# A gated mix of a spectral filter and a gelu layer on one core: the instruction order as a list of steps, gate weights by GpSimd's queue, no zero products

## The chip, the cores and the metric

The kernel runs on one core of one Trainium2 chip. The metric is the device time of one execution in microseconds (us); a lower time is better. A kernel is timed in several runs, and its median counts. Besides, one execution is profiled; that execution has a time of its own, and its span (from the first to the last instruction) is a little shorter than this time.

The engines are called as the profile calls them: PE (TensorE, matrix products), PEld (its weight loads, which run beside the products), DVE (VectorE), ACT (ScalarE), POOL (GpSimd) and SP (SyncE, which only issues transfers). SP, ACT and POOL each have a queue from which transfers start.

## The reference, cut to what matters

```
def _A_ref(x, w_r, w_i):            # x: 1 x 2048 x 512
    X = rfft2(x, axes=(-2, -1))
    X = X * (w_r + 1j * w_i)        # 2048 x 257
    return irfft2(X, s=(2048, 512), axes=(-2, -1))

def _B_ref(x, w1, b1, w2, b2):      # w1: 512 x 1792, w2: 1792 x 512
    return gelu(x @ w1 + b1) @ w2 + b2

g = sigmoid((x * gate_w).sum(-1, keepdims=True))
out = g * _A_ref(x) + (1 - g) * _B_ref(x)
```

All arrays are float32.

## The kernel before, in words

**Products with split operands.** PE multiplies in a rounded float format. To keep float32 accuracy most operands are split: `h` is the operand rounded to 12 bits (an ACT copy), `l` is the rest (a DVE subtraction), and a product is made as hh + hl + lh, three PE instructions. A 128x512 tile product is one PE instruction of 512 columns. So behind almost every PE result stand an ACT and a DVE instruction before PE can use it again.

**The spectral half.** The 2048 rows are taken as 16 groups `j` of 128. For each `j` the function `forward` folds the row (`eo`, `w`, on DVE), makes the transform along the 512 columns by PE (`pd`, with the table `cf`, lines 676-685), splits the result (`zb`, lines 695 and 698), and makes the first transform step along the rows (`py`, with `tf`, lines 705-715). The two columns of the table `cf` that are left over carry the gate weights, so the same `pd` product gives the gate's logit; a tile `g3` holds the gate weights, and five tiny DVE instructions turn it into the columns of `cf` (lines 614-622). The rest of the transform along the rows, the filter and the way back are radix-4 steps on DVE (`radix4`, `filt`, `stage4`; lines 756-868); one small product `pown` (line 742) stands between them. `inverse` scales by the gate (`tg`), mixes the two halves (`pq` on DVE, line 901), multiplies (`pz`, `pa`) and adds the result.

**The gelu half.** Columns `c` = 0 and 1 of the row groups go through `mlp`: twelve 512-column products into a PSUM tile `ph` (line 1007 and after), gelu on ACT (line 995), the split into `g..h` and `g..l` (lines 557, 558), and three products per weight tile into `po`. This is done in passes over the 14 blocks `f` of the hidden layer; sums of the passes are added in DRAM by an adding transfer on POOL's queue (line 498). Columns 2 and 3 go through `fast`, which saves products by a seven-product scheme (Strassen's kind): `nu` and `ux` are its PSUM tiles, and `ux` is written by an ACT copy first and then added to by PE (line 1185). Before these copies, two products with a zero operand (`zerob`, lines 1168-1171) fill the two `ux` tiles once.

**PSUM.** There are eight tiles of one bank: four of kind `pf` (`pd`, `nu`, `pz`, `pa`) and four of kind `pm` (`ph`, `po`, `py`, `ux`). A tile that is given to a new owner waits for the last reader of the old one.

**What sets the order.** All work is first recorded as 2016 steps, each with an engine, the tiles that it reads and writes, a cost and a lag. `Graph.schedule` then plays a list scheduler: whenever an engine is free it takes, of the steps whose inputs are there and for whose tiles a buffer is free, the one with the lowest rank. The ranks are a table of numbers (`RANKS`), and `most` limits how many buffers a class of tiles holds. Costs, lags, a reserve of 0.4 for what PE waits for (`SPARE`) and a look ahead of 0.35 (`AHEAD`) take part. The plan gives every step its place and every tile its buffer number. The steps are then written out in this order, each engine gets its own in this order, and on the chip each engine goes through its list one by one: an instruction that waits holds up all that stand behind it on its engine.

**The start.** SP issues the first weight tile `war0` (two halves), the gate weights (`g3`, line 600), the second row tile `xf4` (two halves), and so on; ACT's queue issues the first row tile `xf0`. PE runs products on a zero tile (`none`) until data is there: six of 512 columns and `FILL` = 8 of 256 columns (lines 573-587).

Of the kernel before, what the change touches and what calls it, by code (L numbers as in the profile page):

```python
# [11 lines left out]
F32 = mybir.dt.float32  # L12
F32R = mybir.dt.float32r
AF = mybir.ActivationFunctionType
ALU = mybir.AluOpType
# [104 lines left out]
SPARE = 0.4  # L120

AHEAD = {"vec": 0.35, "act": 0.35}
# [5 lines left out]
RANKS = """  # L128
# [78 lines left out]
"""  # L207


# [1168 lines left out]
```

## Time and profile before

| what | value |
|---|---|
| median of 3 runs | 367.2 us (366.71 to 367.24) |
| the profiled execution, its own time | 368.04 us |
| its span | 366.2 us |
| busy: PE, DVE, ACT, POOL | 358.7, 327.8, 256.7, 69.6 us |
| granted TensorE clock, mean | 0.999 |
| moved by the 16 DMA engines | 70.35 MB, 192 GB/s in the mean |

How to read it: "busy" is the union of an engine's instructions. PE's instructions overlap in a pipeline, so a row of one product reads 0.39 us while the next one starts 0.227 us later; what a product costs is the distance to the next. A row of the timeline has the start, the duration, the engine, the line, the operation, the tiles (output<-input, without buffer numbers) and how often it stands there in a row; an idle time before it and what ended it may follow. A row of the waits has the engine and line that waited, what it waited for, and the sum in us, the number of times and the longest. A row of the windows has the busy time and the number of instructions of each engine in a stretch, then the granted clock, the share of the DMA engines and GB/s.

### The profile page before, as it was taken

The page shows a single profiled execution, that of the slowest core. Times are in us where ns is not written, and L with a number is a line of the kernel's source. Part 1 is how long each engine was busy: PE and PEld are TensorE (multiplying, and loading weights), DVE is VectorE, ACT ScalarE, POOL GpSimd, SP SyncE. Part 2 cuts the span into 40 slices and gives each one's busy share as a digit, 9 for nine tenths or more (in the row PEclk, how much of TensorE's full clock was granted, in tenths as well). Part 3 has the DMA queues.
Part 4 walks back from the last instruction along what each step waited for, and adds up shares of the span by engine and source line. Part 5 has one row for each costly group of instructions (what it writes and reads, how often), then busy time and mean ns, then how long its engine had stood idle before and what let it go on. Part 6 is the DMA issues. An engine that isn't in the chain of part 4 may idle for free.

```text
span 366.2 us, 5746 instructions
## 1 busy us (share of the span) xinstructions
PE 358.7 (98%) x1808; PEld 302.9 (83%) x1808; DVE 327.8 (90%) x746; ACT 256.7 (70%) x471; POOL 69.6 (19%) x89
## 2 busy tenths in 40 slices
PE   8999999999999999999999999999999999999994
PEld 8888898898878778878888788888888888888884
DVE  5999988998759999899999999999999769899962
ACT  4985778789986241753759975999999998655200
POOL 0210001100211311410333100002333112121220
PEclk9999999999999999999999999999999999999999
DMA  7999785647885937999999943339887637799896
GB/s 224 306 322 303 253 233 166 106 149 233 206 204 129 189 58 155 273 263 365 196 153 217 264 85 117 86 122 225 126 141 150 100 64 156 173 296 241 199 250 184
DMA packets 46719, 70.35 MB, mean 192 GB/s; under 512 B 5600, under 2 KB 19424, under 8 KB 46688
## 3 DMA queue, kind: packets, MB, share of 16 engines
q1 hardware_dynamic: 34880, 48.93, 41.8%
q0 software_dynamic: 11376, 20.71, 35.3%
q10 hardware_dynamic: 432, 0.33, 0.3%
q8 instruction: 14, 0.23, 0.3%
q14 instruction: 17, 0.14, 0.1%
HBM read 48.32 MB, written 19.41 MB: 185 GB/s over the span
## 4 chain that ended last, share of the span: by engine, by line
PE 75%; DVE 12%; DMA 5%; ACT 4%; issue 2%; SPq 1%; DVEq 0%; ACTq 0%
PE poB L507 20%; PE po L507 13%; PE ph L507 11%; PE ux L1185 9%; PE nu L1185 7%; PE pd L507 4%; PE pz L507 3%; PE py L507 3%; PE pa L507 3%; DVE m L856 3%; DMA wf<-in_wf 3%; DMA y<-ownr 1%; DMA xf<-in_xt 1%; DVE y L760 1%; DVE y L758 1%
## 5 line engine op out<-in xcount | busy, mean ns | idle before, releaser
L995 ACT ACTIVATE ph<-ph,b1t 128x512 f32<-128x512 f32 x28 | 18.4, 658 | 25.5 <-PE ph L507 25.2
L498 POOL DMA_DIRECT2D bacc<-o x16 | 15.3, 1029 | 43.2 <-ACT o L1073 43.2
L894 ACT ACTIVATE sw<-y,al 64x512 f32<-64x512 f32 x32 | 22.8, 718 | 0.6
L498 POOL DMA_DIRECT2D bacc<-oB x16 | 13.9, 889 | 43.0 <-ACT oB L1073 33.7
L856 DVE TENSOR_TENSOR m<-y,wf 128x514 f32<-128x514 f32 x32 | 20.7, 688 | 0.0
L507 PE MATMUL pd<-cf,w 128*128 128x129 f32 x128 | 17.7, 276 | 0.0
L507 PEld LDWEIGHTS pz<-tg,pq 128*128 128x128 f32 x128 | 16.8, 191 | 1.1
L507 PEld LDWEIGHTS pd<-cf,w 128*128 128x128 f32 x128 | 16.6, 191 | 1.2 <-DVE zb L698 0.3
L1185 PE MATMUL nu<-xf,wa0h 128*128 128x512 f32 x56 | 17.3, 390 | 0.0
L507 PE MATMUL pz<-tg,pq 128*128 128x128 f32 x128 | 17.2, 274 | 0.0
L507 PE MATMUL py<-zb,tf 128*128 128x258 f32 x96 | 17.1, 295 | 0.0
L723 ACT ACTIVATE y<-pys 64x257 f32<-64x257 f32 x32 | 13.2, 417 | 3.9 <-DVE pys L720 3.4
L507 PE MATMUL pa<-zb,ci 128*128 128x256 f32 x96 | 15.2, 285 | 0.2 <-ACT od L935 0.2
L507 PEld LDWEIGHTS pa<-zb,ci 128*128 128x128 f32 x96 | 13.8, 189 | 1.9 <-ACT od L935 0.7
L507 PEld LDWEIGHTS py<-zb,tf 128*128 128x128 f32 x96 | 14.1, 190 | 1.2 <-ACT pys L716 0.2
L1073 ACT ACTIVATE o<-po 128x512 f32<-128x512 f32 x16 | 9.2, 593 | 8.3 <-PE po L507 8.2
L901 DVE SCALAR_TENSOR_TENSOR pq<-y,al,sw 128x256 f32<-128x256 f32 x32 | 14.4, 479 | 0.0
L695 ACT ACTIVATE zb<-pd 128x256 fp32r<-128x256 f32 x32 | 11.6, 384 | 3.9 <-PE py L507 3.9
L698 DVE TENSOR_TENSOR zb<-pd,zb 128x256 fp32r<-128x256 f32 x32 | 12.5, 417 | 1.1 <-ACT zb L695 1.1
L665 DVE TENSOR_TENSOR w<-eo 128x256 f32<-128x256 f32 x32 | 12.8, 418 | 0.0
L662 DVE TENSOR_TENSOR eo<-xf 128x256 f32<-128x256 f32 x32 | 12.4, 419 | 0.0
L1185 PEld LDWEIGHTS nu<-xf,wa0h 128*128 128x128 f32 x56 | 10.5, 188 | 2.2
(701 smaller groups left out, 1274.3 us busy)
## 6 DMA issues: line engine op xcount, KB each, us to landing
wf<-in_wf SPq DMA_DIRECT2D x16, 257.0 KB, 4.7
bacc<-o POOLq DMA_DIRECT2D x16, 256.0 KB, 6.1
bacc<-oB POOLq DMA_DIRECT2D x16, 256.0 KB, 4.9
xf<-in_xt SPq DMA_DIRECT2D x14, 256.0 KB, 5.0
wr<-in_w SPq DMA_DIRECT2D x14, 256.0 KB, 4.9
tf<-tf SPq DMA_DIRECT2D x16, 192.0 KB, 2.8
bacc<-o SPq DMA_DIRECT2D x8, 256.0 KB, 3.2
ba<-bacc SPq DMA_DIRECT2D x8, 256.0 KB, 4.1
```

The source lines that it names most:

```text
L498: return add("pool", 2.3 * kb / 340, 3.4, lambda: nc.gpsimd.dma_start(dst(), src(), accum_op=ALU.add), reads, writes, rank)
L507: pe.matmul(ps, w, x, start=start, stop=stop)
L662: v(lambda s=s, op=op: vec.tensor_tensor(eo.ap()[:, s], x.ap()[:, 0:2], x.ap()[:, 2:4], op=op), 256, [x], [(eo, s)], feed)
L665: v(lambda s=s, op=op: vec.tensor_tensor(w.ap()[:, s], eo.ap()[:, :, 0], eo.ap()[:, :, 1], op=op), 256, [eo], [(w, s)], feed)
L695: a(lambda c=c: act.activation(segs(xh, c), both(c), AF.Copy), 256, [ps[c]], [(xh, c)], 0)
L698: v(lambda c=c: vec.tensor_tensor(segs(xl, c), both(c), segs(xh, c), op=ALU.subtract), 256, [ps[c], (xh, c)], [(xl, c)], 0)
L723: a(lambda o=o, i=i: act.activation(Y[j].ap()[o:o + HP, 1], pys.ap()[i:i + HP, 1], AF.Copy), 257, [(pys, 1)], [(Y[j], 1 + k)], 0, more=0.1)
L856: v(lambda mk=mk, k=k, y=y, w=w: vec.tensor_tensor(mk.ap(), y.ap(), w.ap()[:, k:k + 1, :ND].to_broadcast([P, 2, ND]), op=ALU.mult), 514, [ ...
L894: a(lambda sw=sw, y=y, o=o, i=i: act.activation(sw.ap()[o:o + HP], y.ap()[i:i + HP, ::-1, :HD], AF.Copy, scale=al.ap()[i:i + HP, 0:1]), 51 ...
L901: v(lambda sw=sw, pq_=pq_, y=y, j=j, k=k, op=op: vec.scalar_tensor_tensor(pq_.ap()[:, k], y.ap()[:, k, :HD], al.ap()[:, 1 + j:2 + j], sw.a ...
L995: a(lambda: act.activation(ps.ap(), ps.ap(), AF.Gelu_apprx_tanh, bias=b1t.ap()[:, f:f + 1]), 600, [b1t], [ps]).table = "gelu"
L1185: pe.matmul(o.ap(), w(wi, e), FX[j].ap()[:, xi, e], start=first, stop=k == 5, skip_group_check=not start)
```

## The change

The list scheduler goes, with `RANKS`, `most`, `SPARE` and `AHEAD`. In its place stand two tables: `ORDER`, the numbers of the 2015 steps in the order in which they are written out, and `SLOTS`, the buffer number of each tile. `schedule` now only gives out these numbers and asserts that every step comes after those it needs and that a buffer is free when it is given away. The order is another one throughout, on every engine; the products, copies and transfers in it are the same but for these:

- the gate weights `g3` and the bias `b1t` are issued by POOL's queue instead of SP's;
- `FILL` is 10 instead of 8: two more products on the zero tile at the start;
- the two products with a zero operand into `ux` go, and the clearing of `zerob` on DVE with them.

The changed costs and lags (0.4, 3.0 and so on) only stand in the records; with a fixed order nothing reads them.

```diff
-RANKS = """
-0 12 294 321 326 399 330 333 323 340 343 1 13 7 14 20 23 11 35 26 10 2 5 8 19 4 32 56 47 53 78 22 42 73 43 45 21 25 72
...
+ORDER = """
+0 2 15 13 1 22 16 14 19 23 24 508 25 506 26 27 3 527 4 37 17 18 5 6 7 109 8 9 38 10 554 34 530 39 11 65 12 543 64 507
...
+SLOTS = """
+0 0 0 1 2 5 6 0 0 0 0 0 32 0 1 0 0 3 0 2 2 3 0 1 27 1 2 1 0 3 3 3 40 0 1 3 0 0 1 0 0 0 0 2 20 2 2 0 3 2 6 30 30 4 9 3
...
-    def schedule(self):
...
+    def schedule(self, order, slots):
+
+        bufs = []
         for s in self.steps:
...
             for b in s.bufs:
                 if b.slot is None:
...
+                    b.slot = next(slots)
+                    assert b.slot < self.slots[b.tag]
+                    bufs.append(b)
+        held, done = {}, []
+        for n in order:
+            s = self.steps[n]
+            assert s.need == 0
+            for b in s.bufs:
+                last = held.setdefault((b.tag, b.slot), b)
+                assert last is b or last.left == 0
+                held[b.tag, b.slot] = b
+            for q in s.after:
+                q.need -= 1
+            for b in s.bufs:
+                b.left -= 1
+            done.append(s)
+        assert len(done) == len(self.steps)
+        return done
...
-    FILL = 8
+    FILL = 10
...
-    dma(lambda: sp.dma_start(gw.ap().rearrange("p a b -> p (a b)"), x0g[:, NQ * P:]), 8, [], [gw], 0.5)
+    add("pool", 0.1, 3.5, lambda: nc.gpsimd.dma_start(gw.ap().rearrange("p a b -> p (a b)"), x0g[:, NQ * P:]), [], [gw], 0)
...
-        dma(lambda: sp.dma_start(b1t.ap(), b1), 7, [], [b1t], 0.45)
+        add("pool", 0.1, 4.0, lambda: nc.gpsimd.dma_start(b1t.ap(), b1), [], [b1t], 0.1)
...
-            zero = buf("w", [P, P], F32R, "zerob", cls="zero")
-            add("vec", 0.3, 0.1, lambda: vec.memset(zero.ap().bitcast(F32), 0.0), [free[CA[1]]], [zero])
-            for x in free["X"]:
-                m(lambda x=x: mm(x.ap(), zero.ap(), bcast(zero.ap(), 4), True, True), 512, 1, [zero], [x])
...
-    ranks = RANKS.split()
-    assert len(ranks) == len(g.steps)
-    for s, r in zip(g.steps, ranks):
-        s.rank = 0.05 * int(r)
-    order = g.schedule()
+    order = g.schedule([int(n) for n in ORDER.split()], iter([int(n) for n in SLOTS.split()]))
```

Three places show what the new order moves. The rows are instructions of one engine in their order, with the line, the operation, the output and inputs with their numbers in the program, the shape, and how many equal ones follow each other.

**The start of SP's queue.** `war` are w1's tiles, `wb..l_raw` w2's, `xf` row tiles, `g3` the gate weights, `b1t` the bias, `cf` the transform's table. Before, from the first transfer on:

```order
L981 DMA war0_80<-in_w1 128x256 x2
L600 DMA g3_99<-in_x0g 128x4
L596 DMA xf4_101<-in_xt 128x256 x2
L984 DMA war1_104<-in_w1 128x512
L968 DMA wb0l_raw_106<-in_w2 128x512
L625 DMA b1t_112<-in_b1 128x14
L569 DMA xf8_120<-in_xt 128x512
L569 DMA xf12_128<-in_xt 128x512
L602 DMA cf_137<-cf 128x258
L968 DMA wb1l_raw_142<-in_w2 128x512
L968 DMA wb2l_raw_153<-in_w2 128x512
L602 DMA cf_137<-cf 128x258
```

Now, from the first transfer on:

```order
L505 DMA xf4_90<-in_xt 128x256 x2
L890 DMA war0_97<-in_w1 128x256 x2
L893 DMA war1_105<-in_w1 128x512
L478 DMA xf8_110<-in_xt 128x512
L478 DMA xf12_112<-in_xt 128x512
L893 DMA war3_123<-in_w1 128x512
L877 DMA wb1l_raw_127<-in_w2 128x512
L893 DMA war2_134<-in_w1 128x512
L877 DMA wb4l_raw_142<-in_w2 128x512
L877 DMA wb0l_raw_149<-in_w2 128x512
```

and after one more w2 tile (`wb2l_raw`):

```order
L893 DMA war4_157<-in_w1 128x512
L511 DMA cf_174<-cf 128x258
L1001 DMA xb000xe_176<-in_xc 128x512
L538 DMA al_183<-al 128x17
L511 DMA cf_174<-cf 128x258
```

The row tiles `xf8` and `xf12` move from the 9th and 10th transfer of this queue to the 6th and 7th; the second half of `cf` moves from the 14th to the 18th.

**The start of PE.** `none` are the products on the zero tile, `ph0_0` and `ph0_1` the first two blocks of the hidden layer. Before:

```order
L507 MATMUL none_92<-zero_74 128x512 x6
L507 MATMUL none_92<-zero_74 128x256 x7
L507 MATMUL ph0_0_130<-mxh00_114,wa0h_109 128x128 x2
L507 MATMUL none_92<-zero_74 128x256
L507 MATMUL ph0_0_130<-mxh00_114,wa0h_109 128x128 x6
L507 MATMUL ph0_0_130<-mxl00_134,wa0h_109 128x256 x4
```

Now:

```order
L416 MATMUL none_76<-zero_74 128x512 x6
L416 MATMUL none_76<-zero_74 128x256 x10
L416 MATMUL ph0_0_139<-mxh00_108,wa0h_137 128x128 x8
L416 MATMUL ph0_0_139<-mxl00_129,wa0h_137 128x256 x4
L416 MATMUL ph0_1_178<-mxh00_108,wa1h_154 128x256 x4
```

All ten short fill products now stand ahead of the first product with data. A little further on, the first `pd` products now stand behind the whole of `ph0_2` (twelve 512-column products) and no longer ahead of it.

**DVE around the first inverse.** `pq2` is what the first `pz` product (`pz2`) multiplies, made in two halves by line 901 (810 in the changed file). Before, the second half:

```order
L1142 TENSOR_TENSOR wr9_2659<-wr8_2577,wr9_2659 128x256
L558 TENSOR_TENSOR g3_4l_2860<-ux1_2303,g3_4h_2849 128x512
L901 SCALAR_TENSOR_TENSOR pq2_2786<-y_536,al_318,sw2_2761 128x256
L901 SCALAR_TENSOR_TENSOR pq6_2871<-y_536,al_318,sw6_2781 128x256
L901 SCALAR_TENSOR_TENSOR pq10_2879<-y_536,al_318,sw10_2796 128x256
```

Now, both halves:

```order
L1051 TENSOR_TENSOR wr7_2175<-wr6_2225,ws3_2595 128x256
L669 SCALAR_TENSOR_TENSOR d3u3_2814<-y_508 128x256
L810 SCALAR_TENSOR_TENSOR pq2_2821<-y_508,al_183,sw2_2776 128x256 x2
L1099 TENSOR_TENSOR ux1_2362<-ux1_2362,five2_2681 128x512
L667 TENSOR_TENSOR d3u2_2804<-y_508 128x256
```

Fewer DVE instructions stand ahead of `pq2`: 117 of 128x256 where there were 123, 86 of 128x512 where there were 91, 38 of 2x256 columns where there were 42, and 2 of 128x128 where there were 5. On PE `pz2` moves forward too: 855 products of 512 columns stand ahead of it where there were 881 (two of these are the zero products).

More of the change, by code (lines that the diff above doesn't have):

```diff
@@ L1 @@
-import heapq
 import math
@@ L116, in _tables @@
     return tuple(np.ascontiguousarray(t, np.float32) for t in (cf, ci, tf, ti, fx, al))
-SPARE = 0.4
-AHEAD = {"vec": 0.35, "act": 0.35}
 PSUM = ("pf", "pm")
-RANKS = """
[78 rows of a table removed]
+ORDER = """
[78 rows of a table added]
+"""
+SLOTS = """
[18 rows of a table added]
 """
@@ L220, in __init__ @@
         self.t = self.raw = None
-        self.seq = None
     def ap(self):
@@ L253, in __init__ @@
         self.need = 0
-        self.open = 0
-        self.there = 0.0
         self.table = None
-        self.at = None
 class Graph:
-    def __init__(self, slots, most):
-        self.slots, self.most = slots, most
-        self.order = {}
+    def __init__(self, slots):
+        self.slots = slots
         self.steps = []
@@ L299, in add @@
             d.after.append(s)
-        s.need = s.open = len(deps)
+        s.need = len(deps)
         for b in s.bufs:
             b.left += 1
-            if b.seq is None:
-                b.seq = self.order.get(b.cls, 0)
-                self.order[b.cls] = b.seq + 1
         self.steps.append(s)
         return s
-    def schedule(self):
-        ready = {}
-        soon = {e: [] for e in AHEAD}
-        table = None
-        free = {t: list(range(n)) for t, n in self.slots.items()}
-        held_by = {c: 0 for c in self.order}
-        nxt = {t: 0 for t in self.order}
-        busy = {}
-        wire = 1.3
-        events = []
-        done = []
-        def push(s):
-            heapq.heappush(ready.setdefault(s.eng, []), (s.rank, s.n, s))
-        for s in self.steps:
-            if s.need == 0:
-                push(s)
-        now = 0.0
-        n = 0
-        def takes(s):
-            want = {}
+    def schedule(self, order, slots):
+        bufs = []
+        for s in self.steps:
@@ L337, in takes @@
             for b in s.bufs:
                 if b.slot is None:
-                    want.setdefault(b.cls, []).append(b)
-            for k, bs in want.items():
-                if (sum(len(o) for c, o in want.items() if c[0] == k[0]) > len(free[k[0]]) or
-                        held_by[k] + len(bs) > self.most.get(k, 1000) or
-                        sorted(b.seq for b in bs) != list(range(nxt[k], nxt[k] + len(bs)))):
-                    return None
-            return [b for bs in want.values() for b in bs]
@@ L427, in schedule @@
-        assert len(done) == len(self.steps), "steps that never start"
-        self.span = now
-        return sorted(done, key=lambda s: (s.at, s.n))
+                    b.slot = next(slots)
[14 more added lines that the diff above has]
+            done.append(s)
@@ L448, in tile_kernel @@
     whole = ("ttab", "xhl", "w", "ctab")
-    most = {("pm", "ph"): 2, ("pm", "po"): 2, ("pm", "po0"): 1, ("pm", "py"): 3, ("pf", "nu"): 4, ("t2k", "pq"): 2, ("w", "g"): 12, ("w", "gB"): 16,
[3 rows of a table removed]
-    g = Graph(slots, most)
+    g = Graph(slots)
     add = g.add
@@ L593, in tile_kernel @@
     for k in range(2):
-        dma_act(lambda k=k: act.dma_start(x0.ap()[:, 2 * k:2 * k + 2].rearrange("p a b -> p (a b)"),
-                                          x0g[:, k * HD:(k + 1) * HD]), 128, [], [(x0, k)])
+        add("act", 0.4, 3.0, lambda k=k: act.dma_start(x0.ap()[:, 2 * k:2 * k + 2].rearrange("p a b -> p (a b)"),
+                                                       x0g[:, k * HD:(k + 1) * HD]), [], [(x0, k)], 0)
         add("sp", 128 / 340, 2.4, lambda k=k: sp.dma_start(x4.ap()[:, 2 * k:2 * k + 2], xt[4][:, 2 * k:2 * k + 2]), [], [(x4, k)],
@@ L957, in inverse @@
             if late:
-                acc(lambda w=w: w.ap(), lambda k=k: ba[k].ap(), 256, [ba[k]], [w])
+                add("pool", 2.3 * 256 / 340, 5.0, lambda w=w, k=k: nc.gpsimd.dma_start(w.ap(), ba[k].ap(), accum_op=ALU.add), [ba[k]], [w])
                 dma(lambda w=w, k=k: sp.dma_start(
@@ L980, in load_w @@
                 o = slice(k * HD, (k + 1) * HD)
-                add("sp", 128 / 340, 1.9 + 0.3 * k, lambda o=o: sp.dma_start(t.ap()[:, o], src[:, o]), [], [(t, k)])
+                add("sp", 128 / 340, 1.4 + 0.2 * k, lambda o=o: sp.dma_start(t.ap()[:, o], src[:, o]), [], [(t, k)])
                 v(lambda o=o: vec.tensor_copy(h.ap()[:, o], t.ap()[:, o]), 256, [(t, k)], [(h, k)])
```

78 lines of the change are left out of this document (removed), and 174 rows, old and new, of tables (ORDER, RANKS, SLOTS, most).

## The prediction, written before the changed kernel ran

> **What bounds the kernel now.** I read the page first: the engines' shares, the slices and the shares of the chain.
>
> ```profile
> span 366.2 us, 5746 instructions
> PE 358.7 (98%) x1808; PEld 302.9 (83%) x1808; DVE 327.8 (90%) x746; ACT 256.7 (70%) x471; POOL 69.6 (19%) x89
> ...
> PE   8999999999999999999999999999999999999994
> ...
> PE 75%; DVE 12%; DMA 5%; ACT 4%; issue 2%; SPq 1%; DVEq 0%; ACTq 0%
> ```
>
> PE is full in all slices but the first and the last. The products themselves hardly change, so a new order can only win the time in which PE stands still. The chain that ended last runs 12% over DVE, but there PE has other products to do (slices of 9 throughout), so a faster DVE alone wins little. Next I read the waits, those of the weight loads, since a product waits with its load:
>
> ```profile
> PEld none L507 <- DVE zero L575: 1.1, 1, 1.1
> PEld ph L507 <- DVE g_10l L558: 0.9, 1, 0.9
> PEld ph L507 <- ACT mxh L650: 0.8, 1, 0.8
> PEld ph L507 <- DVE g_6l L558: 0.8, 1, 0.8
> PEld pa L507 <- ACT od L935: 0.7, 1, 0.7
> PEld ph L507 <- DVE g_8l L558: 0.4, 1, 0.4
> PEld ph L507 <- issue: 0.4, 1, 0.4
> PEld pown L507 <- issue: 0.4, 1, 0.4
> PEld po L507 <- DMA wb0l<-in_w: 0.3, 1, 0.3
> ```
>
> That is nearly the whole stake: without the first (the start, which stays) 4.7 us, 1.3% of the span. The largest shows what kind of waits they are:
>
> ```profile
> 161.48 0.60 ACT L557 ACTIVATE g_10h<-ph 128x512 fp32r<-128x512 f32 x1
> 162.11 1.89 DVE L856 TENSOR_TENSOR m<-y,wf 128x514 f32<-128x514 f32 x3
> 163.93 0.68 DVE L558 TENSOR_TENSOR g_10l<-ph,g_10h 128x512 fp32r<-128x512 f32 x1
> 164.66 0.50 PE L507 MATMUL ph<-mxh,wa12h 128*128 128x512 f32 x1 [0.51 <-DVE g_10l L558]
> ```
>
> ACT had g_10h ready at 162.1, but three filter products stood ahead of g_10l on DVE, and the PSUM tile that PE wanted came free only after it. It is the order that makes this wait, with no engine short of time.
>
> **The change part by part**, on the span.
>
> The zero products:
>
> ```profile
> L507 PE MATMUL ux<-zerob x2: 389/389/389, 188.6 to 191.6; 128*128 128x512 f32 x2
> 192.63 1.36 PE nu L1185 x6
> ```
>
> Six products of 512 columns take 1.36 us, so one costs 0.227; two that go, in a stretch where PE is full: **-0.45 us**. If PE waits there in the new order anyway, 0.
>
> Two more fill products, and the start:
>
> ```profile
> 1.06 4.42 PE L507 MATMUL none<-zero 128*128 128x512 f32 x13 [1.06 <-DVE zero L575]
> 5.28 0.52 PE L507 MATMUL ph<-mxh,wa0h 128*128 128x128 f32 x2
> 9.22 0.65 PE L507 MATMUL ph<-mxh,wa1l 128*128 128x256 f32 x4
> 10.50 0.74 PE L507 MATMUL ph<-mxh,wa1h 128*128 128x256 f32 x4 [0.64 <-ACT mxh L650]
> 13.48 0.72 PE L507 MATMUL pd<-cf,w 128*128 128x129 f32 x5
> 0.74 0.86 SPq L981 DMA_DIRECT2D war<-in_w  x2
> 3.06 0.43 SPq L984 DMA_DIRECT2D war<-in_w  x1
> 4.99 4.81 DMA xf<-in_xt
> 9.82 0.64 ACT mxh L650
> ```
>
> The 13 fills fill 1.06 to 5.28; six long ones count double, so a short one is 4.22/19 = 0.22 us. Two more: **+0.44**, the bound below is 0, if they run where PE would wait. PE then waits again at 10.50, for the row tile xf12. SP issues every 0.47 us (0.74 to 3.06 for five); xf12 moves from the 10th to the 7th transfer, 1.4 us earlier (to 3.56), lands at 8.4 by the same 4.81, and is copied by ACT at 9.0. PE comes there at about 9.7 + 0.44, so the wait goes: four products of 0.12 after 9.22 end at 9.70, up to 10.50 it is **-0.8**. The two weights of the gate and the bias that leave SP's queue are a part of this 1.4 us. On POOL's queue they cost its time, and POOL was idle until 11.29 but for small clearings:
>
> ```profile
> 11.29 1.01 POOL L498 DMA_DIRECT2D wb0l<-in_w  x1 [10.30 <-DMA rev<-in_wrev]
> DMA to landing us min/median/max: 3.3/5.4/9.1
> ```
>
> The second row is POOL's transfers of line 498. Issued by 1.8, the gate weights land between 5.1 and 7.2 at the smallest and the median time. The first DVE instruction on them stands 9th, behind eight that take DVE to about 6; behind it wait the l parts of the later row tiles, which PE needs only after 9. Cost 0, at most 1.
>
> What is late next is cf. Its second half moves from the 14th to the 18th transfer of SP:
>
> ```profile
> 0.00:10.00 10.00, 8.80 (x42) 7.87 (x42) 5.38 (x16) 4.74 (x9) 0.47 (x10) 1.00 0.73 230
> 10.00:20.00 10.00, 9.50 (x62) 8.49 (x63) 9.90 (x30) 9.87 (x21) 2.74 (x3) 1.00 1.08 298
> cf<-cf SPq DMA_DIRECT2D x2, 129.0 KB, 4.7
> ```
>
> PE now reaches the first pd after ph0_2: 13.48 + 0.44 - 0.8 + 12 x 0.227 = 15.8. By issue (0.74 + 17 x 0.47 = 8.7) and 4.7 to land, cf is there at 13.4: no wait. By bytes it is later: 15 tiles of 0.26 MB, 3.9 MB in all; 230 GB/s bring 2.3 MB in the first 10 us, and at 298 the other 1.6 MB take 5.5 us: 15.5. Then a tiny DVE copy of 0.2. So 0 to, if the rate is a tenth lower, +1.5; I take **+0.3**, near the bytes, since the engines were at a share of 1.08 there. The Trainium skill bears on this (Trainium Kernel Development and Optimization, Key Constraints): transfers from SP, ACT and POOL all run on the same 16 DMA engines, and issuing from several queues saves only the issue time. By it the move to POOL's queue brings no byte earlier and the time by bytes is the right one, so the sum keeps its +0.3 or more; by issue times alone it would lose that term. The share of 1.08 in the second row agrees with it.
>
> The waits after the start. Of the list above they are 0.9 + 0.8 + 0.7 + 0.4 + 0.4 + 0.4 + 0.3 = 3.9 us. In the new order ph1_12 gets the PSUM tile of ph0_12, 30 products (6.8 us) after that was full, and no longer that of ph1_10, 15 products (3.4 us) after; ph1_8 gets that of a po, which only an ACT copy has to leave. So the two largest lose their cause. New ones can arise: nothing in the trace shows their number. The bounds are none (-3.9) and as many as now (0), with a loss in the third rival. I take half: **-2.0**, because the small ones of 0.3 to 0.4 are what the handover costs wherever two engines come out even.
>
> The end:
>
> ```profile
> 361.21 0.28 PE L507 MATMUL poB<-g_13h,wb13lb 128*128 128x256 f32 x1
> 361.52 0.42 DVE L1266 TENSOR_TENSOR oB<-y,poB 128x256 f32<-128x256 f32 x1 [0.23 <-PE poB L507]
> 361.97 0.33 SPq L1269 DMA_DIRECT2D out<-oB  x1
> 353.73 0.86 POOL L498 DMA_DIRECT2D w<-ba  x1 [0.62 <-DVE oB L1266]
> ```
>
> Before, the last half of 256 columns is subtracted and stored; now the half that is stored in two quarters comes last. It ends two DVE instructions later instead of one, with smaller transfers: 0, within 0.3. SP now has the store of the last added tile (w101) just ahead of its last transfer. Its addition was issued 7.5 us before the last product; POOL's longest landing is 9.1, the median 5.4, so it could hold SP up by 1.6 at the worst.
>
> Sum: -0.45 + 0.44 - 0.8 + 0.3 - 2.0 = **-2.5 us**. The profiled execution's own time, 368.04, would be 365.5 (span 363.7). The median of the runs is 0.84 below that execution; so the median becomes **364.7**.
>
> **The rivals.**
>
> *Nearly all waits go.* The whole 3.9 and the 0.8, with no wait for cf: -0.45 + 0.44 - 0.8 - 3.9 = -4.7, so 362.5. For it: no PE wait in the list is a lack of an engine's time but in the start. Against it: PE meets ACT and DVE at hundreds of places, and a plan that never misses by 0.3 us would need to know each landing.
>
> *The waits change places.* The -2.0 becomes 0 and the start gains nothing, as cf takes back the 0.8: -0.45 + 0.44 = 0, so 367.2. For it: the kernel has only 1.3% to lose, and each order has its own misses.
>
> *DVE is late for the first inverse*, the one on the slower side:
>
> ```profile
> 220.00:240.00 20.00, 20.00 (x90) 16.57 (x89) 19.93 (x42) 16.05 (x27) 0.88 (x1) 1.00 0.30 93
> 239.34 1.27 DVE L901 SCALAR_TENSOR_TENSOR pq<-y,al,sw 128x256 f32<-128x256 f32 x3
> 242.41 1.05 PE L507 MATMUL pz<-tg,pq 128*128 128x128 f32 x8
> ```
>
> From 220 to 240 DVE is busy for 19.93 of 20 us, and it is the filter's chain that PE must have before pz2. In the new order 26 products less stand ahead of pz2; without the zero products these are 24 x 0.227 = 5.4 us. With the -2.2 of the terms so far PE comes there at about 242.4 - 5.4 - 2.2 = 234.8. DVE made pq2's second half by 239.7. Ahead of it now stand 6 fewer instructions of 256 columns (0.42 in the rows above) and 9 fewer of 512 (0.68), at most 8.6 us, and 3 small ones; as neighbours overlap a little I take 8.0, so 231.7. It leads by 3.1 us, about as before (242.4 - 239.7 = 2.7). But that needs DVE to stay as busy: its filter chain waits for tiles of wf, and what it loses there beyond 3.1 us PE loses one for one. If DVE came only when it did before, PE would wait 239.7 - 234.8 = 4.9: -2.5 + 4.9, so 369.6. Against it: the lead did not shrink. For it: the DMA queues of the filter (wf, 4.7 us to land) stand in another order too, and a fixed list cannot react.
>
> **How the numbers follow.** My forecast has 0.50, nearly all waits gone 0.17, changed places 0.13, DVE late 0.20. The forecast's own range is 363.3 to 366.2 (half of the 3.9 either way, cf at 0 to 1.5). The whole range is **362.2 to 368.5**: it takes in the second case with a little of the fills hidden, and the slower case up to half its wait; left out are about 0.06 below and 0.12 above. What a measurement can tell is 0.2%, 0.7 us. Faster: 0.50 less 0.01 for a forecast that ends above its range, 0.17, and 0.03 of the third case: 0.69. The same: 0.09 of the third case and 0.01 each of the first and the last: 0.11. Slower: 0.19 of the late DVE and 0.01 of the third case: 0.20.
>
> **What would show it.** The rows ux<-zerob gone, and no PE wait for mxh near 10 us. The first pd at 15.5 to 16.5, with a wait for cf or w if the bytes decide. No wait of ph for g_10l near 160. pz near 235, with no wait for pq. PE busy less and the sum of PEld waits after the start between 1.5 and 3. I am wrong if this sum stays at 4 or above, if PE waits for pq or for tiles of wf's chain by more than 1 us at one place, or if SP's last transfer starts over 1 us after the last product because w101 was late.

## The result, and the profile after

| | median us | range, runs |
|---|---|---|
| before | 366.81 | 365.54 to 368.2, 22 |
| changed | 365.87 | 364.9 to 368.71, 22 |

The ratio is 0.9987, with a 95% interval of 0.9971 to 1.0003: no change that this measurement can tell. It is the ratio of the means (366.77 and 366.28); the medians alone would give 0.9974, but three runs of the changed kernel at 368.2 to 368.7 pull its mean up. The forecast was 364.7, 0.7% under the 367.2 shown then. The result lies inside both of its ranges, near their slow side, but the gain that was forecast is not there, and "the same" had only 0.11.

The page of the changed kernel, with the lines that answer to those of before:

```profile
span 363.9 us, 5723 instructions
PE 357.3 (98%) x1808; PEld 302.3 (83%) x1808; DVE 331.2 (91%) x745; ACT 254.2 (70%) x471; POOL 70.5 (19%) x91
...
PE   8999999899999999999999999999999999999996
...
PE 89%; DVE 4%; DMA 2%; ACT 2%; issue 1%; SPq 0%; DVEq 0%; ACTq 0%
```

The span is 2.3 us shorter than that of the execution before, near the -2.5 of the forecast, yet the medians differ by 0.9. The profiled execution before took 368.04, 1.2 more than its own kernel's median over 22 runs; the one after took 365.88, its median. So two spans cannot be compared here without asking how each stands to its median. One slice in PE's row, the eighth (64 to 73 us), has an 8 now where there was a 9. The waits of the weight loads say what stands there ("issue" means that the profile shows nothing that was waited for):

```profile
PEld po L416 <- DVE g_4l L467: 1.4, 1, 1.4
PEld none L416 <- DVE zero L484: 1.1, 1, 1.1
PEld ph L416 <- issue: 0.8, 2, 0.4
PEld ph L416 <- DVE mxl L560: 0.5, 1, 0.5
PEld pd L416 <- PE pd L416: 0.5, 1, 0.5
PEld py L416 <- ACT zb L604: 0.4, 1, 0.4
PEld poB L416 <- ACT oB L982: 0.4, 1, 0.4
PEld pown L416 <- issue: 0.4, 1, 0.4
PEld pz L416 <- PE poB L416: 0.3, 1, 0.3
```

g_10l, g_6l, g_8l, od and mxh are gone from the top, as forecast. But the eight largest rows without the fills' 1.1 come to 4.7 us, just what the eight largest came to before. The timeline of the changed kernel shows the places (start, duration, engine, line, operation, and in brackets the idle time ahead with what ended it):

```profile
1.65 0.91 SPq L890 DMA_DIRECT2D war<-in_w  x2
...
5.81 0.50 DVE L891 CAST wa0h<-war 128x256 fp32r<-128x256 f32 x2 [0.44 <-DMA war<-in_w]
...
6.25 1.14 PE L416 MATMUL ph<-mxh,wa0h 128*128 128x128 f32 x8
...
13.42 0.40 PE L416 MATMUL ph<-mxh,wa2h 128*128 128x512 f32 x1
...
16.17 0.61 PE L416 MATMUL pd<-cf,w 128*128 128x129 f32 x4
...
56.71 0.63 ACT L472 ACTIVATE wa10l<-wa10h 128x512 fp32r<-128x512 f32 x1
...
58.14 0.15 DVE L608 TENSOR_REDUCE logit<-pd 128x1 f32<-128x2 f32 x1
...
58.32 0.39 ACT L604 ACTIVATE zb<-pd 128x256 fp32r<-128x256 f32 x1 [0.98 <-DVE logit L608]
...
63.10 0.15 DVE L608 TENSOR_REDUCE gate<-pd 128x1 f32<-128x2 f32 x1
...
63.28 0.66 ACT L604 ACTIVATE zb<-pd 128x256 fp32r<-128x256 f32 x2 [0.98 <-DVE gate L608]
...
65.22 0.66 ACT L904 ACTIVATE ph<-ph,b1t 128x512 f32<-128x512 f32 x1
...
67.74 0.68 DVE L467 TENSOR_TENSOR g_4l<-ph,g_4h 128x512 fp32r<-128x512 f32 x1
...
68.47 0.50 PE L416 MATMUL po<-g_4l,wb4h 128*128 128x512 f32 x1 [0.96 <-DVE g_4l L467]
...
77.01 0.16 DVE L608 TENSOR_REDUCE gate<-pd 128x1 f32<-128x2 f32 x1 [0.50 <-ACT zb L604]
...
234.34 0.87 DVE L810 SCALAR_TENSOR_TENSOR pq<-y,al,sw 128x256 f32<-128x256 f32 x2
...
236.12 1.05 PE L416 MATMUL pz<-tg,pq 128*128 128x128 f32 x8
...
360.13 0.28 PE L416 MATMUL poB<-g_13h,wb13lb 128*128 128x256 f32 x1
...
360.76 0.33 SPq L1169 DMA_DIRECT2D out<-oB  x1
360.97 0.35 ACTq L1169 DMA_DIRECT2D out<-oB  x1
```

The rows of 58 and 63 us are the strange ones. ACT stands still for 0.98 us twice and goes on 0.03 us after DVE has ended a sum of two columns of a `pd` tile into `logit` or `gate`. ACT's waits for such sums are these two and a third one of 0.49 at 52.66:

```profile
ACT zb L604 <- DVE logit L608: 1.5, 2, 1.0
ACT zb L604 <- DVE gate L608: 1.0, 1, 1.0
```

In the kernel before no copy `zb` waits for a sum. The copy `zb` that ACT wants to make does not use that sum: both only read the same `pd` tile in PSUM. ACT loses 2 us, the gelu of block 4 comes at 65.22, g_4l at 67.74, and PE stands still at 68.47. At 77.01 it is the other way round: DVE waits with a sum for ACT's copy.

**Three stretches.** For all profiles the time is cut in three: up to the end of the first two hidden blocks (the start of the product that follows ph0_0 and ph0_1: 13.42 above, 13.48 before), from there to the start of the last product (360.13 above, 361.21 before), and on to the end of the span. The last column is the profiled execution's own time.

| run | two blocks done | to the last product | to the end | own time |
|---|---|---|---|---|
| before | 13.48 | 347.73 | 5.0 | 368.04 |
| before_again | 13.53 | 346.28 | 3.9 | 365.54 |
| before_third | 14.07 | 345.67 | 4.7 | 366.19 |
| changed | 13.42 | 346.71 | 3.8 | 365.88 |
| after_again | 14.13 | 346.74 | 3.7 | 366.58 |
| start_swapped | 13.62 | 346.59 | 3.7 | 366.06 |
| small_on_sp | 13.16 | 346.87 | 4.0 | 365.75 |
| fills_two | 14.67 | 346.27 | 3.8 | 366.69 |
| extra_twelve | 13.81 | 348.93 | 3.8 | 368.50 |
| reads_first_two | 13.86 | 345.69 | 3.8 | 365.30 |
| reads_first_two_timed | 13.69 | 345.12 | 3.7 | 364.52 |
| reads_swapped | 13.35 | 344.71 | 3.7 | 363.82 |
| waits_repaired | 13.60 | 344.40 | 3.8 | 363.82 |
| repaired_and_war0 | 13.01 | 344.99 | 3.8 | 363.89 |

The middle column of the kernel before varies by 2 us between three profiles, that of the changed kernel by 0.03 between two. That is no rule: reads_first_two and reads_first_two_timed are one program, and they differ by 0.57. So differences of a few tenths in this column, between single profiles, show nothing.

### The profile page after: what moved, and what is told of

The parts are those of the page before. It is cut to its first block, busy times and chain, and to the rows that moved or that the text cites. A ratio compares the mean times of both kernels' runs of the same rounds, so it can differ in the third digit from the quotient of the medians.

```text
span 363.9 us, 5723 instructions
## 1 busy us (share of the span) xinstructions
PE 357.3 (98%) x1808; PEld 302.3 (83%) x1808; DVE 331.2 (91%) x745; ACT 254.2 (70%) x471; POOL 70.5 (19%) x91
## 4 chain that ended last, share of the span: by engine, by line
PE 89%; DVE 4%; DMA 2%; ACT 2%; issue 1%; SPq 0%; DVEq 0%; ACTq 0%
PE poB L416 21%; PE po L416 20%; PE ph L416 18%; PE ux L1090 11%; PE nu L1090 8%; PE pz L416 4%; PE pa L416 3%; PE pd L416 2%; PE py L416 2%; DMA tf<-tf 1%; DMA war<-in_w 1%; DVE w L574 1%; ACT zb L604 1%; DVE eo L571 1%; DVE mxl L560 0%
## 5 line engine op out<-in xcount | busy, mean ns | idle before, releaser
L407 POOL DMA_DIRECT2D bacc<-o x16 | 14.5, 949 | 55.0 <-ACT o L982 55.0
L416 PE MATMUL pd<-cf,w 128*128 128x129 f32 x128 | 18.3, 275 | 0.4 <-DVE zb L607 0.4
L416 PEld LDWEIGHTS pz<-tg,pq 128*128 128x128 f32 x128 | 17.1, 191 | 1.6 <-PE poB L416 0.3
L416 PEld LDWEIGHTS pd<-cf,w 128*128 128x128 f32 x128 | 16.9, 190 | 1.5 <-PE pd L416 0.5
L416 PE MATMUL pz<-tg,pq 128*128 128x128 f32 x128 | 17.6, 275 | 0.0
L416 PE MATMUL py<-zb,tf 128*128 128x258 f32 x96 | 16.9, 294 | 0.2 <-DMA tf<-tf 0.2
L416 PEld LDWEIGHTS py<-zb,tf 128*128 128x128 f32 x96 | 14.0, 189 | 1.6 <-ACT zb L604 0.4
L822 ACT ACTIVATE zb<-pz 128x512 fp32r<-128x512 f32 x16 | 9.5, 597 | 7.1 <-PE pz L416 7.1
L416 PEld LDWEIGHTS pa<-zb,ci 128*128 128x128 f32 x96 | 13.3, 188 | 1.1
L416 PE MATMUL pa<-zb,ci 128*128 128x256 f32 x96 | 13.6, 280 | 0.0
```

The lines of the kernel that those rows point to most:

```text
L407: return add("pool", 2.3 * kb / 340, 3.4, lambda: nc.gpsimd.dma_start(dst(), src(), accum_op=ALU.add), reads, writes, rank)
L416: pe.matmul(ps, w, x, start=start, stop=stop)
```

## The experiments

Two theories stood at the start. A: the waits belong to the order; the new order took old ones away and made new ones, of which the largest come from two engines that read one PSUM tile. B: the profiled execution before was a long one, and a part of the waits that the prediction wanted to win was chance.

### The same kernels again

before_again and before_third are the kernel before, after_again the changed one, with no edit.

> A second profile of the kernel before, unchanged. Theory A (the waits that the prediction summed belong to the order): PE waits again for g_10l 0.6 to 1.0, mxh 0.6 to 0.9, g_6l 0.5 to 0.9 and od 0.5 to 0.8, the list without the fills' 1.1 again comes to 4.2 to 5.2, and the last product ends at 361.2 to 361.8. Theory B (the profile of before was one of its long executions, 368.04 where the median is 366.81, and the waits were longer for that): own time 366.3 to 367.2, the list comes to 3.0 to 4.0, the last product ends 0.7 to 1.5 earlier, and at least two of the four named waits are under half.

> A third profile of the kernel before. If its waits near 60-75 and 120-133 us come from late landings (ownr and wf: DVE waited 5.1 us for them in the first profile and 1.0 in the second), then the stretch from the first pd to the last product, 347.7 and 346.3 so far, goes with DVE's waits for transfers: under 2 us of these give 346.0 to 346.6, over 4 give 347.4 to 348. The waits for g_10l (0.7 to 0.9) and od (0.5) come again either way.

> A second profile of the changed kernel, unchanged. Theory A: the new waits belong to the new order and come again: po for g_4l 1.0 to 1.5 near 68, pd for zb 0.4 to 0.7 near 77.7, mxl 0.4 to 0.7 near 10.4; last product at 360.1 to 360.7. Theory B: the names and sizes change, the three sum to under 1.2 us, and the last product moves by over 0.5.

Neither theory holds alone. Before, DVE's waits for transfers in the first profile:

```profile
DVE wf L851 <- DMA wf<-in_wf: 3.5, 3, 2.1
...
DVE b0d L758 <- DMA y<-ownr: 2.6, 1, 2.6
```

In before_again:

```profile
DVE wf L851 <- DMA wf<-in_wf: 2.1, 2, 1.7
...
DVE b0d L758 <- DMA y<-ownr: 0.5, 1, 0.5
```

In before_third only the first of them is left:

```profile
DVE wf L851 <- DMA wf<-in_wf: 1.7, 2, 1.1
```

The sums of 6.1, 2.6 and 1.7 us go with 347.73, 346.28 and 345.67 of the middle stretch. Behind a DVE that waits for `ownr` or `wf` stand the l parts that PE wants (g_6l was made at 123.36 in the first profile, at 121.09 and 121.55 in the others); in the two later profiles the rows for g_6l and g_8l are missing from PE's waits:

```profile
PEld ph L507 <- ACT mxh L650: 1.2, 1, 1.2
...
PEld ph L507 <- DVE g_10l L558: 1.0, 1, 1.0
PEld pa L507 <- ACT od L935: 0.7, 1, 0.7
```

That is before_again; mxh, g_10l and od stay, as A had it, and g_6l and g_8l go. Not all went as B had it: of the four named waits only g_6l fell under half, where it asked for two, the own time of 365.54 lies below its 366.3, and the eight largest rows still come to 5.0, since mxh at the start grew. The third profile missed two bounds: 345.67 is under the 346.0 to 346.6, and g_10l waited 0.4 instead of 0.7 to 0.9. The wait for mxh is not fixed either (0.8, 1.2, 1.8). That the landings make the middle stretch longer is read from these three profiles; no edit tested it. In the changed order they seem not to: in its two profiles DVE waits 1.1 and 3.2 us for `ownr` and `wf`, and the middle stretch is 346.71 and 346.74.

In after_again the new waits came back: g_4l 1.4, pd 0.5, mxl 0.5, py 0.3, and ACT waits for the two sums by 1.0 each. So they belong to the order. The last product ended at 361.15, outside A's 360.1 to 360.7 and moved by over 0.5 as B had it, but nearly all by the start (0.71 later): the middle stretch is 346.74 against 346.71. wa0h could be cast only at 6.51, since the first weights landed later:

```profile
6.51 0.49 DVE L891 CAST wa0h<-war 128x256 fp32r<-128x256 f32 x2 [0.81 <-DMA war<-in_w]
...
6.96 1.08 PE L416 MATMUL ph<-mxh,wa0h 128*128 128x128 f32 x8 [0.86 <-DVE wa0h L891]
```

### Who may read a PSUM tile first

The edit of reads_swapped moves four steps of the list, the first of each pair to the place right behind the second:

```diff
-    order = g.schedule([int(n) for n in ORDER.split()], iter([int(n) for n in SLOTS.split()]))
+    todo = [int(n) for n in ORDER.split()]
+    for n, k in ((232, 228), (255, 252), (324, 323), (349, 350)):
+        todo.remove(n)
+        todo.insert(todo.index(k) + 1, n)
+    order = g.schedule(todo, iter([int(n) for n in SLOTS.split()]))
```

232 and 255 are the sums whose end released ACT at 58 and 63 us, 228 and 252 ACT's copies; 324 and 349 are two sums with which DVE waited for ACT's copy, at 77.0 and 78.4.

> Four one-column sums of a pd tile (DVE, into gate and logit) move one or a few places down the list, behind the copy of the same tile (two of them behind ACT's, two behind DVE's second half); nothing else changes. Theory A (two engines that read one PSUM tile take turns in the order of the list, so a sum listed ahead makes ACT's copy wait for DVE): ACT's copies at 58.3 and 63.3 no longer wait about 1 us each, PE's wait for g_4l near 68 falls from 1.2-1.4 to under 0.4, the pd wait near 77.7 from 0.5 to under 0.2, the last product ends 1.1 to 1.7 us earlier than in the changed kernel (358.7 to 359.3), the median is 1.0 to 1.7 below it. Rival (reads of one tile run side by side and ACT was late for another reason): the copies start when they did, nothing moves by more than 0.3 us.

Median 364.26 (363.82 to 364.68), 0.9937 of the kernel before, interval 0.9918 to 0.9956. The middle stretch fell by 2.0 to 344.71; the last product ended at 358.3, below the 358.7 to 359.3 expected, so the rival (nothing moves by more than 0.3) is out. The largest waits that are left:

```profile
PEld none L416 <- DVE zero L484: 1.1, 1, 1.1
PEld ph L416 <- issue: 0.7, 2, 0.4
PEld pd L416 <- issue: 0.4, 2, 0.2
PEld poB L416 <- ACT oB L982: 0.4, 1, 0.4
```

reads_first_two has only the first two pairs.

> Only the two sums that stand ahead of ACT's copies at 58.3 and 63.3 are put behind them. If these two make the wait for g_4l and the other two the wait of pd near 77.7: the wait for g_4l is gone (from 1.24 to under 0.3), the pd wait near 77 stays at 0.4 to 0.6, and the last product lies 0.9 to 1.4 earlier than in a changed kernel with the same start. If one cause stood behind both, the pd wait would go too.

Both pairs are neighbours in the list and belong to different engines, so no instruction changes its place on any engine. What changes are waits: the copy no longer waits for the sum, and the sum now waits for the copy. For the copies, each row of ACT with its waits, the changed kernel's (-) and this one's (+):

```
-L604 ACTIVATE zb_88<-pd_831 128x2x128 [waits DVE_49]
+L604 ACTIVATE zb_88<-pd_831 128x2x128 [waits PE_49]
-L604 ACTIVATE zb_99<-pd_877 128x256 [waits DVE_49]
+L604 ACTIVATE zb_99<-pd_877 128x256 [waits PE_49]
```

In its timeline ACT's copies follow the instruction ahead of them without a wait, and the wait for g_4l is gone:

```profile
57.30 0.63 ACT L472 ACTIVATE wa10l<-wa10h 128x512 fp32r<-128x512 f32 x1
57.83 0.37 ACT L604 ACTIVATE zb<-pd 128x256 fp32r<-128x256 f32 x1
...
61.82 0.66 ACT L604 ACTIVATE zb<-pd 128x256 fp32r<-128x256 f32 x2
...
67.94 0.39 PE L416 MATMUL po<-g_4l,wb4h 128*128 128x512 f32 x1
```

The pd wait near 77 stayed at 0.5 (`PEld pd L416 <- PE pd L416: 0.5, 1, 0.5` again), as it should if the other two sums make it. The middle stretch fell by 1.0.

> reads_first_two once more, timed. No instruction changes its place on any engine; only what two of ACT's copies wait for is another. If that alone is worth the 1.0 us that its profile showed from the end of the first two blocks to the last product (346.7 to 345.7): again 345.4 to 346.0 there, and a median of 364.6 to 365.3, between 365.87 of the changed kernel and 364.26 of reads_swapped. If the first profile was chance: 346.4 to 347.0 and 365.6 or more.

Median 364.67 (12 runs), 0.9957 of the kernel before, interval 0.9935 to 0.998; the middle stretch 345.12, 0.3 below its bound. What two copies wait for, with nothing moved, is worth 0.3% by these ratios (0.9957 against the 0.9987 of the changed kernel). The two intervals overlap by a little (0.998 and 0.9971); that of reads_swapped, with all four sums moved, lies wholly below that of the changed kernel.

The Trainium skill (PSUM — Partial Sum Buffer, "PSUM bank collisions raise a hardware error") says that two engines must not touch one bank in the same quadrant at once, two readers included, so that the compiler puts a dependency between any two such instructions. The waits above agree, with 0.98 us for each copy and 0.03 us from the end of one reader to the start of the next.

### The start

start_swapped puts war0 back ahead of xf4 on SP's queue, and DVE's sum of row tile 12 behind that tile's l part, by the same loop:

```diff
+    for n, k in ((116, 121), (16, 506), (14, 16)):
```

> The changed kernel with the two halves of war0 ahead of the two halves of xf4 on SP's queue again, and on DVE the l part of row tile 12 ahead of that tile's sum eo. If the order of these makes the waits at the start: the first ph starts when the fills end (5.8 to 5.9, was 6.25), the wait for mxl near 10.4 falls from 0.53 to 0.1-0.25, and the first pd comes 0.5 to 0.8 us earlier. Rival (the start is bound by landings): xf4, 0.9 us later, takes the place of war0, ph0_1 waits for its mxh or mxl, and the first pd comes within 0.2 us of before.

The rival was right that nothing is won. The first ph came at 5.91, but the second half of its eight products waited for the mxh of xf4, now the later one (0.3 in the list of weight loads), wa1l took 0.5, the two blocks were done at 13.62, inside the range of 13.35 to 14.13 that the changed order has without the edit, and the first pd came at 16.45, 0.28 later than in the changed kernel and so a little outside the rival's 0.2. Here its weights also waited for the copy into cf (0.3 in the list).

fills_two lets eight of the ten short fills emit nothing:

```diff
-    for _ in range(FILL):
-        add("pe", 0.22, 0.0, lambda: mm(...
+    for k in range(FILL):
+        add("pe", 0.22, 0.0, lambda k=k: k < 2 and mm(...
```

> The changed kernel with 2 of its 10 short fill products (the first of them); 8 x 0.213 = 1.7 us of products less. If the fills are hidden behind the landing of war0: the first ph starts when wa0h is there, at 6.0 to 7.0 as in the two profiles of the changed kernel (6.25, 6.96), and the time stays within 0.7 of 366. If they are on the path, the first ph starts at 4.5 and the time falls by 1.7. A third way: PE stands still for 2 us ahead of the first ph, its clock is released later, the first twelve products take up to 1.3 us longer, and the time rises by that.

The row of the first products with data:

```profile
6.73 1.94 PE L416 MATMUL ph<-mxh,wa0h 128*128 128x128 f32 x8 [2.32 <-DVE wa0h L891]
```

1.7 us of fills less, and nothing was won: PE stood still for 2.32 us until the weights came. The eight products then took 1.94 us, where they took 1.14 in the changed kernel, and the two blocks were done 0.5 to 1.3 later than in its two profiles; the middle stretch was 0.4 shorter, which may be chance, so that the time shows little of it. So the fills are hidden, as the first of the three ways had it, and the products behind them go faster for them, as the third had it.

small_on_sp issues the gate weights and the bias from SP again:

```diff
-    add("pool", 0.1, 3.5, lambda: nc.gpsimd.dma_start(gw.ap()...
+    add("sp", 0.1, 3.5, lambda: sp.dma_start(gw.ap()...
...
-        add("pool", 0.1, 4.0, lambda: nc.gpsimd.dma_start(b1t.ap(), b1)...
+        add("sp", 0.1, 4.0, lambda: sp.dma_start(b1t.ap(), b1)...
```

> The changed kernel with one part undone: gate weights and bias again issued by SP, as its 3rd and 8th transfer, the rest as listed. If the issue time of SP sets the start: wa0h is cast 0.47 later (6.2 to 7.0, was 5.7 to 6.5 in the changed kernel), the first ph and the end of the first two hidden blocks 0.47 later too (13.9 to 14.6, was 13.35 to 14.13). If the landing of the bytes sets it: both within the range of the changed kernel, so that the move to GpSimd's queue is worth nothing. From the end of these two blocks to the last product 346.5 to 346.9 as in the two profiles of the changed kernel.

wa0h was cast at 5.54, the two blocks were done at 13.16, earlier than in any run of the changed order. The move to GpSimd's queue is worth nothing that shows inside the span; SP's issue time does not set the start. Outside the span it seems to cost: the own time is 1.95 to 2.06 above the span in 22 runs of the changed kernel, 1.73 to 1.84 in 50 runs of the kernel before, and 1.75 here, with both transfers back on SP. That is 0.2 us; that this move makes them rests on one run, and why is open.

### The zero products

extra_twelve puts twelve products ahead of the first nu product, whose own first one overwrites them:

```diff
                 def emit():
                     k = 0
+                    if p == 0 and A is W0[0] and i == "11":
+                        for _ in range(12):
+                            pe.matmul(o.ap(), w(0, 0), FX[j].ap()[:, 0, 0], start=True, stop=True)
```

> Twelve products of 512 columns are added in front of the first nu product, about where the two zero products stood (their result is overwritten by the product that follows). If PE is full there, as the prediction took it: 12 x 0.227 = 2.7 us later at the last product, so that two cost 0.45. If PE has slack there: under 1.4, and the PE waits behind this place shrink by the rest.

The added products and the first that the kernel itself has there, at 179.6 and so 9 us ahead of where the zero products stood:

```profile
179.55 2.88 PE L1090 MATMUL nu<-xf,wa0h 128*128 128x512 f32 x12
182.27 0.62 PE L1094 MATMUL nu<-xf,wa0h 128*128 128x512 f32 x2
```

From the first row's start to the second's is 2.72. The last product starts 2.61 later than in the changed kernel (362.74 against 360.13), the first ph 0.39 later. Of these 2.61 the start has 0.39, so the middle stretch is longer by 2.22 (348.93 against 346.71), 0.185 a product where each takes 0.227. So most of what a product takes there is paid at the end, as PE being full has it, and the two zero products were worth 0.37 to 0.45.

### Versions that beat both

waits_repaired is reads_swapped with nine more steps moved (the expectation says ten):

```diff
-    for n, k in ((232, 228), (255, 252), (324, 323), (349, 350)):
+    for n, k in ((232, 228), (255, 252), (324, 323), (349, 350), (178, 149), (665, 321),
+                 (116, 121), (60, 116), (33, 60), (29, 556), (31, 29), (30, 31), (32, 30)):
```

> The four sums as in reads_swapped, and ten more steps moved in the list: at the start on DVE three sums eo behind the l part of row tile 12, and the small chain from the gate weights to cf two instructions earlier; on ACT one copy zb ahead of a y near 45 and one copy of wa6 behind two zb near 75. If PE's waits are made by the order: the waits at 8.9 and 10.4 fall from 0.3 and 0.42-0.59 to under 0.2 each, py near 45.9 from 0.33-0.46 to under 0.2, and the last product ends 0.4 to 1.0 earlier than in reads_swapped (357.3 to 357.9 with the same first ph); median 363.4 to 364.0. If each repair makes a new wait nearby: within 0.3 of reads_swapped, 364.0 to 364.6.

Median 363.68 (363.38 to 363.86), 0.9928 of the kernel before, interval 0.9907 to 0.9949. The waits at 8.9, 10.4 and 46 are gone, and a smaller one for wa2l (0.3) is new: from the first ph the two blocks took 6.23 us (7.37 to 13.60) where the changed order takes 7.17. But the first ph came at 7.37, since the weights landed late in this execution, so that the last product ended at 358.28, level with reads_swapped.

repaired_and_war0 issues war0 first as well:

```diff
-                 (116, 121), (60, 116),
+                 (16, 506), (14, 16), (116, 121), (60, 116),
```

> waits_repaired, and the halves of war0 ahead of the halves of xf4 on SP's queue. With the l parts first on DVE the first two blocks took 6.2 us from the first ph, which started at 7.4 for a late war0. If war0's place makes the late start: first ph at 5.9 to 6.0, then waits for xf4's mxh of 0.4 to 0.8, the two blocks done at 12.6 to 13.1 (13.60 in waits_repaired), last product at 356.9 to 357.6, median 0.4 to 0.9 under waits_repaired. If xf4 then makes up for it: done at 13.3 or later, median within 0.3 of 363.7.

Median 363.30 (362.82 to 363.89), 0.9915, interval 0.9897 to 0.9932. The first ph came at 5.76 and the two blocks were done at 13.01, in the range expected; the last product ended at 358.27, above the one expected, because a wait for g_11l appeared that waits_repaired does not have (0.6 in the list of weight loads, as in after_again). It is the fastest of all, but its interval overlaps that of waits_repaired: the last 0.4 us are not shown.

## Why the prediction was wrong

The step that failed is the -2.0 for the waits after the start. With the zero products the middle stretch was to fall by 2.45; it is 346.7 in two profiles of the changed kernel and 346.6 in the mean of three of the kernel before. Of the three stretches only the end is shorter, 3.75 against 4.5 in the means of the same profiles, and there the forecast had 0.

**The zero products, -0.45.** Right within 0.1: extra_twelve gives 0.37 to 0.45.

**The fills, +0.44, and mxh, -0.8.** Together they were to bring -0.36 at the end of the first two blocks. Three profiles before give 13.48 to 14.07, six with the changed order at the start (changed, after_again, extra_twelve and the three of the reads) 13.35 to 14.13, with means of 13.69 and 13.71: nothing. The fills are hidden, and the wait for mxh is gone, but in their place PE waits for wa0h. The second step that failed is "What is late next is cf". Late next was war0, the first weights: the new order issues them behind xf4, their two halves are cast from 5.81 on, and the first ph moves from 5.28 (4.78 in before_again, 4.68 in before_third) to 6.25 (6.96 in after_again). In before_again:

```profile
3.34 0.29 DVE L982 CAST wa0h<-war 128x256 fp32r<-128x256 f32 x1 [2.34 <-DMA war<-in_w]
...
4.11 0.29 DVE L982 CAST wa0h<-war 128x256 fp32r<-128x256 f32 x1 [0.47 <-DMA war<-in_w]
...
4.78 0.34 PE L507 MATMUL ph<-mxh,wa0h 128*128 128x128 f32 x2
```

In all nine profiles with xf4 issued ahead of war0, the first ph starts 0.44 to 0.45 after the first cast of wa0h starts, so this cast releases it and the fills do not. From the first ph on the new order is faster, 7.17 us to the end of the two blocks where the first profile before has 8.20; the late weights took that back (0.97). The order rows shown ahead of the prediction show war0 move behind xf4, and the sum has no term for it. Its place alone is not the cause, though: with war0 first again (start_swapped) xf4 is late and nothing is won.

**cf, +0.3.** Nothing, but near: pd follows ph0_2 at 16.17 without a wait, and DVE's copy into cf began at 15.69, just when the time by bytes (15.5 and the copy) had it.

**Gate weights and bias on GpSimd's queue, 0.** Right inside the span, by small_on_sp. Outside it 0.2 us were lost that the forecast did not have, as it took the distance from span to own time as fixed.

**The waits after the start, -2.0.** This term failed twice over. First, the stake of 3.9 us was read from one execution, 1.2 above its kernel's median. The waits for g_6l and g_8l, 1.2 us together, are in that execution, with DVE's longest waits for transfers, and two more profiles do not have them. And then the 0.84 by which the execution was longer than the median was taken off once more. As far as it was made of these waits, which their size suggests and nothing proves, the prediction won them twice. Against the first profile the middle stretch did fall, by 1.0 with the zero products in it. Against the other two it rose by 0.4 to 1.1. Second, "nothing in the trace shows their number" was said of the new waits, and half of the stake was kept as a guess. The places could have been read beforehand, not their cost: the built program says for each instruction what it waits for, and ACT's two copies waited for DVE there. But such an order need not cost anything: of the 32 sums 27 ran ahead of ACT's copy of their tile in the kernel before and held none up, 18 did in the changed one and held up three. With these two pairs and the two sums near 77 put right the kernel is 1.6 us faster than the changed one (364.26 against 365.87), and the 0.6% that it then has over before (0.9937) is close to the 0.7% that was forecast. That closeness is luck, since the terms behind it are others: 344.71 in the middle against 345.67 to 347.73 before, and the end. The order was worth it; four steps in it gave most of it back.

**The end, 0 within 0.3.** Mis-sized: from the last product to the end of the span it is 3.7 to 4.0 in every run of the changed program, 3.9 to 5.0 before. The last two transfers are now quarters, issued at 360.76 and 360.97, where before a half was issued last (361.97). That their smaller size makes the end shorter is likely and was not tested. w101 held nothing up.

**The rivals.** That the waits change places (0.13) is what happened in the middle, though by a mechanism that the rival did not name. DVE late for the first inverse did not happen, but it was nearer than forecast: pz2 came at 236.12, and pq2 was ready at 235.2, a lead of 0.9 and not of 3.1. (The -2.2 "of the terms so far" in that working is not their sum, which is -2.5; that is 0.3 of the lead.)

**The signs.** ux<-zerob, mxh and g_10l are gone as said, pd at 16.17 and pz at 236.12 were near their 15.5 to 16.5 and 235. The sign against the forecast was there too: a sum of PE's waits at 4 or above.

## What to carry to other kernels

An order of steps is more than the order on each engine: where two engines read one PSUM tile, the list decides who waits for whom, so read the waits of the built program beside its order, above all those on an engine that the data do not name, and look in a timeline which of them are ever waited out. Before waits are counted as a stake, take a second profile of the same kernel: what an order made here came back in the same rows, while waits that went with late landings did not; and do not subtract an execution's excess over the median from a sum that already wins that excess. Where a transfer moves forward in a queue, cost the one that it passes.

## What the runs showed of the hardware

Readers of one PSUM tile on ACT and DVE took turns: each of the 32 `pd` tiles is read by ACT's copy and DVE's sum, and in the first profiles of the kernel before and of the changed one none of these 64 pairs overlaps; where the second was waiting, it began 0.03 us after the first had ended. The waits that keep them apart stand in the built program; no run here leaves them out.

The first weights, two transfers of 128 KB, began to be cast between 5.54 us (small_on_sp) and 6.93 (waits_repaired) in the runs that issue them behind xf4. This spread of 1.4 us between executions is larger than the 0.94 that the best repair of the start won.

After 2.32 us without products PE took 1.94 us for eight products that take 1.08 to 1.60 in the runs with all fills, while the page's row of the granted clock has a 9 in the first slice of fills_two and of the changed kernel alike: that row does not tell the difference.
